# Linear attention and highway FFN: the last batch's queries turned by two DMA transposes, pair stores by every second partition, two thirds of the step list made anew

## The chip, the cores and the metric

The kernel runs on one core of one Trainium2 chip. The metric is device time in microseconds (us) of one execution. Engines are named as in the profile: PE is TensorE's matmul and PEld its weight load, DVE is VectorE, ACT is ScalarE, POOL is GpSimd, and SP is SyncE, which issues nearly all DMAs. L410 means line 410 of the kernel.

## The reference

```
# q, k, v: (8 batches, 8 heads, 576 positions, 64)
q_s = exp(q - max(q)) / sum over the last axis
k_s = exp(k - max(k)) / sum over the positions
kv  = einsum('bhsd,bhse->bhde', k_s, v)
x   = einsum('bhsd,bhde->bhse', q_s, kv), heads side by side: (4608, 512)
H   = max(x @ w_h, 0)
T   = 1 / (1 + exp(-(x @ w_t + b_t)))
out = T * H + (1 - T) * x          # (4608, 512), float32
```

The kernel leaves out the maxima (they cancel) and divides the query's exponentials only after the product with kv: a column of ones beside kv gives the sum.

## The kernel before

The 4608 rows of the output are 36 tiles of 128 rows. A batch has 576 positions, laid out as 64 partitions with 9 positions each, so two batches share nine tiles: four tiles of one batch, four of the other, and one mixed tile. Tiles 27 to 30 are batch 6, 31 to 34 batch 7, and tile 35, the last, has the ends of both; it is computed in two column halves.

Everything is cut into small steps. A step is one word of a list, ORDER, written out by a planner ahead of time: `xu_31_0` is step xu for tile 31, `:P`, `:A`, `:D` choose the engine, `:F` makes a step take a whole tensor in one instruction. The program issues the steps in that order, and every engine, SP's queue included, takes its own instructions strictly in that order. Waits come only from data and from buffers that are still in use (two PSUM banks each for tps and gps, one each for xu, qps and the turned x; three landing buffers each for q, k and v).

For a batch b:

- `q_b`, `k_b`, `v_b` (L183 to L205): loads in float32 on SP's queue. For batches 4 to 7 the queries come as a main part (`q_b_0`, two DMAs, L198) that fills 128 partitions with eight positions of every head, and the ninth positions (`q_b_9`, L202).
- `ek` (L252) and `vc` (L258): exponentials of k on ACT, the cast of v on any of three engines. `kv` (L268): 72 small matmuls; `kr`, `kn` (L280, L286): division on DVE into kvb.
- `eq` (L297 to L306): exponentials of q on ACT, into a tile qe of 16-bit values. `qt` (L318 or L323): TensorE transposes of qe into the PSUM bank qps, two groups of eight blocks of 128x128 and one small third group. `qc` (L332): a copy from PSUM to SBUF, on DVE or ACT, into eq. `turned_q` names the block of eq that a tile's step xu needs.

For a tile i:

- `xu` (L352): four or eight matmuls of eq's blocks with kvb. `rs`, `x` (L361, L367): division on DVE, giving x in 16 bits. `xt` (L375): four transposes on TensorE. `xe` (L382): their copy to SBUF, on DVE or ACT.
- `bw` puts the bias into a bank of tps, by a matmul (L392) or a copy on ACT (L390). `mt` (L402) adds x @ w_t, `mh` (L410) makes x @ (w_h - 1), four matmuls each.
- `th` (L424, L426): a tanh on ACT. `dd` (L430): a maximum on DVE. `uu`: (tanh + 1) times that, on DVE (L444) or, for `:P`, as two instructions on POOL (L441, L442). `oo` (L462): plus x, on POOL. `st` (L470 to L482): the store.

Tiles are stored in pairs where two neighbours have the same batch (4 KB in a row). For batches 0 to 3 a pair is stored by two DMAs of 256 KB, `st_i_0` from partitions 0 to 63 and `st_i_1` from 64 to 127 (L482). For batches 4 to 6 one DMA of 512 KB takes all 128 partitions (L478); the tiles of batch 7 and the mixed ones are stored alone.

`fill_n` (L167) issues n matmuls on zeros into an unused bank. They stand where TensorE would be idle.

Of the kernel before, what the change touches and what calls it, by code (L numbers as in the profile page):

```python
# [24 lines left out]
xu_4_1 kv_1_0 mt_2_0 kr_1_0 rs_4_1 eq_1_1 bw_5 th_2_0 kn_1_0 xu_5_0 eq_1_2 q_4_0 x_4_1 rs_5_0 x_5_0 mt_5_1 xu_4_0
qt_1_1 qc_1_1:A oo_0_0 v_4_0 xt_5_0 xe_5_0:D mh_5_1 uu_3_0:P bw_4 mh_5_0 rs_4_0 x_4_0 xt_4_1 xe_4_1:D mt_5_0 uu_2_0:P
oo_2_0 eq_2_0:F th_5_0 xu_6_0 dd_5 xt_4_0 xe_4_0:D qt_1_2 mh_4_1 mt_4_1 mt_4_0 th_4_0 oo_3_0 mh_4_0 bw_8:A rs_6_0
uu_5_0:P bw_6:A qc_1_2 ek_2_0:F x_6_0 xt_6_0 xe_6_0:D oo_5_0 xu_8_0 qt_2_0 rs_8_0 mh_6_0 q_4_9 x_8_0 dd_4 xt_8_0
xe_8_0:D xu_7_0 rs_7_0 qc_2_0 x_7_0 mt_6_0 dd_6 mt_8_0 vc_2_2:A qt_2_1 th_6_0 xt_7_0 qc_2_1:A th_8_0 vc_2_0 kv_2_0
mh_8_0 xe_7_0:D uu_6_0 kr_2_0 kn_2_0 mh_7_0 k_4_0 eq_3_0:F xu_9_0 dd_8 uu_4_0:P k_5_0 bw_7 qt_2_2 v_5_0 rs_9_0 oo_4_0  # L30
x_9_0 mt_7_0 xt_9_0 dd_7 qc_2_2:A q_5_0 xu_10_0 xe_9_0:D bw_10:A th_7_0 rs_10_0 x_10_0 oo_6_0 qt_3_0 qc_3_0 mh_9_0
bw_9:A ek_3_0:F uu_8_0:P uu_7_0:P vc_3_0 xu_12_0 st_1_1 xt_10_0 oo_8_0 rs_12_0 x_12_0 xe_10_0:D oo_7_0 mt_9_0 dd_9
qt_3_1 vc_3_2:A xu_11_0 xt_12_0 rs_11_0 x_11_0 xe_12_0:D mt_10_0 th_9_0 th_10_0 kv_3_0 uu_9_0 oo_9_0 xt_11_0 mh_10_0
xe_11_0 kr_3_0 kn_3_0 dd_10 mh_12_0 qc_3_1 xu_14_0 rs_14_0 x_14_0 bw_12:A bw_11:A mt_12_0 mh_11_0 uu_10_0:P oo_10_0
xu_13_0 eq_4_0 eq_4_1 qt_3_2 st_1_0 xt_14_0 vc_4_0 mt_11_0 dd_12 rs_13_0 th_12_0 x_13_0 qc_3_2 uu_12_0:P bw_14:A
oo_12_0 xu_15_0 rs_15_0 x_15_0 xe_14_0 th_11_0 qt_4_0 dd_11 mt_14_0 uu_11_0 xt_13_0 xu_16_0 rs_16_0 qc_4_0:A xe_13_0
x_16_0 mh_14_0 qt_4_1 xt_15_0 th_14_0 bw_13:A xu_17_0 xe_15_0:D mt_13_0 rs_17_0 x_17_0 ek_4_0:F mh_13_0 xt_16_0 eq_4_2
vc_4_2 th_13_0 k_6_0 kv_4_0 dd_14 dd_13 xe_16_0:D kr_4_0 kn_4_0 bw_15:A uu_13_0 mh_15_0 ek_5_0:F bw_16:A oo_11_0
vc_5_2:A mt_15_0 th_15_0 q_5_9 qc_4_1 xu_18_0 rs_18_0 x_18_0 v_6_0 dd_15 uu_14_0:P mh_16_0 xt_17_0 xe_17_0:D qt_4_2
mt_16_0 th_16_0 vc_5_0 dd_16 kv_5_0 oo_14_0 oo_13_0 kr_5_0 kn_5_0 qc_4_2:A mh_17_0 xt_18_0 xe_18_0:D bw_17:A uu_16_0  # L40
q_6_0 mt_17_0 eq_5_0:F xu_20_0 rs_20_0 mh_18_0 st_5_0 qt_5_1 x_20_0 dd_17 xt_20_0 bw_18:A st_3_1 th_17_0 xu_21_0
st_3_0 xe_20_0:D mt_18_0 qc_5_1:A uu_15_0:P bw_20:A rs_21_0 oo_15_0 st_5_1 x_21_0 qt_5_0 xt_21_0 dd_18 q_7_0 v_7_0
th_18_0 bw_21:A st_7_1 oo_16_0 xu_19_0 ek_6_0 uu_17_0:P oo_17_0 xe_21_0:D ek_6_2 rs_19_0 mh_20_0 mh_21_0 vc_6_0:A
x_19_0 xt_19_0 qc_5_0 xe_19_0:D xu_22_0 st_7_0 rs_22_0 x_22_0 dd_20 k_7_0 dd_21 mt_20_0 th_20_0 mt_21_0 vc_6_2
uu_18_0:P xt_22_0 kv_6_0 xe_22_0:D eq_5_2 mh_19_0 bw_19:A mt_19_0 qt_5_2 kr_6_0 kn_6_0 th_21_0 uu_21_0 xu_23_0 qc_5_2
eq_6_0:F mh_22_0 st_16_1 uu_20_0:P qt_6_0 bw_22:A st_10_1 rs_23_0 x_23_0 xt_23_0 xu_24_0 st_10_0 dd_19 mt_22_0
xe_23_0:D oo_18_0 oo_20_0 th_19_0 rs_24_0 oo_21_0 x_24_0 uu_19_0:P bw_23:A dd_22 mt_23_0 oo_19_0 qc_6_0 xt_24_0
xe_24_0:D st_21_0 xu_25_0 mh_23_0 q_6_9 rs_25_0 th_22_0 uu_22_0:P oo_22_0 mh_24_0 x_25_0 xt_25_0 dd_23 xu_26_0 dd_24
# [17 lines left out]
def kernel(  # L66
# [242 lines left out]
    def qt(e, b, g):  # L309
        j0, j1 = GROUPS[g]  # L310
        a, s = (2, 2) if g < 2 else (1, 1)
        t = T[f"qps{b}_{g}"] = ps_q.tile([P, a, 4, s, NP], FP16, tag="qps", name=f"qps_{b}_{g}")
        if b in WIDE and g < 2:
            main = T[f"qe{b}"].rearrange("p j c d -> p (j c d)")[:, 0:MAIN]
            main = main.rearrange("p (hh j kk f) -> p j hh kk f", j=4, hh=2, kk=2)
            for jp in (2 * g, 2 * g + 1):
                for n in range(4):
                    nc.tensor.matmul(t[:, jp % 2, n].rearrange("p s t -> p (s t)"), main[:, jp, n % 2, n // 2], idh,  # L318
                                     is_transpose=True, start=True, stop=True, skip_group_check=True)
# [8 lines left out]
    def qc(e, b, g):  # L328
# [3 lines left out]
        copy(t.rearrange("p a n t -> p (a n t)"), T[f"qps{b}_{g}"].rearrange("p a n s t -> p (a n s t)"))  # L332
# [192 lines left out]
```

## Time and profile before

| what | value |
|---|---|
| median of three runs | 119.64 us (119.22 to 120.39) |
| the profiled execution | 119.67 us |
| its span, first to last instruction | 117.6 us |
| moved by DMA | 40.06 MB, mean 341 GB/s |
| read from and written to HBM | 30.41 MB and 9.44 MB |
| TensorE's clock as granted | 1.000 |

The page has busy time by engine, DMA queues, and the chain of work that ended last, followed back from the last instruction. Other views are asked for with a window, a line or a tile: groups of instructions (busy time in all, mean ns of one, and behind the second bar the idle time of the engine just before them and what ended it), a timeline (start, duration, engine, line, operation), and busy time by windows (length, busy time and count for each engine, granted clock, DMA share, GB/s). Starts are counted from the first instruction of the span.

### The profile page before, as it was taken

The page shows a single profiled execution, that of the slowest core. Times are in us where ns is not written, and L with a number is a line of the kernel's source. Part 1 is how long each engine was busy: PE and PEld are TensorE (multiplying, and loading weights), DVE is VectorE, ACT ScalarE, POOL GpSimd, SP SyncE. Part 2 cuts the span into 40 slices and gives each one's busy share as a digit, 9 for nine tenths or more (in the row PEclk, how much of TensorE's full clock was granted, in tenths as well). Part 3 has the DMA queues.
Part 4 walks back from the last instruction along what each step waited for, and adds up shares of the span by engine and source line. Part 5 has one row for each costly group of instructions (what it writes and reads, how often), then busy time and mean ns, then how long its engine had stood idle before and what let it go on. Part 6 is the DMA issues. An engine that isn't in the chain of part 4 may idle for free.

```text
span 117.6 us, 3461 instructions
## 1 busy us (share of the span) xinstructions
PE 110.6 (94%) x1371; PEld 63.6 (54%) x1371; DVE 94.3 (80%) x223; ACT 92.3 (78%) x130; POOL 91.9 (78%) x103
## 2 busy tenths in 40 slices
...
GB/s 46 393 392 380 408 396 385 378 375 384 394 389 390 389 391 362 374 355 390 389 375 383 381 363 361 395 374 380 406 403 363 279 235 180 301 283 56 210 364 173
DMA packets 22083, 40.06 MB, mean 341 GB/s; under 512 B 3250, under 2 KB 9650, under 8 KB 22068
## 3 DMA queue, kind: packets, MB, share of 16 engines
q1 hardware_dynamic: 21920, 39.72, 94.8%
q8 instruction: 10, 0.16, 0.6%
...
HBM read 30.41 MB, written 9.44 MB: 339 GB/s over the span
## 4 chain that ended last, share of the span: by engine, by line
PE 69%; DMA 17%; DVE 8%; SPq 2%; ACT 1%; issue 1%; DVEq 0%
PE gps L410 23%; PE tps L402 22%; DMA q<-in_q_dram 11%; PE xu L352 6%; DMA v<-in_v_dram 6%; PE turned L375 5%; PE kv L268 4%; DVE x L367 4%; PE qps L323 2%; PE qps L318 2%; SPq L183 2%; PE turned L167 2%; DVE d L430 2%; ACT qe L306 1%; DVE rs L361 1%
## 5 line engine op out<-in xcount | busy, mean ns | idle before, releaser
L462 POOL TENSOR_TENSOR o<-u,x 128x512 f32<-128x512 f16 (+1 forms) x36 | 40.7, 1144 | 3.7 <-DVE u L444 2.8
L402 PE MATMUL tps<-w16t,xT 128*128 128x512 f16 (+1 forms) x148 | 36.3, 373 | 0.8 <-POOL w16t L221 0.8
L410 PE MATMUL gps<-w16h,xT 128*128 128x512 f16 x144 | 36.3, 379 | 0.0
L367 DVE TENSOR_TENSOR x<-xu,rs 128x512 f16<-128x512 f32 (+1 forms) x39 | 25.2, 649 | 2.8
L442 POOL TENSOR_TENSOR u<-g,d 128x512 f16<-128x512 f16 x21 | 24.3, 1157 | 2.5 <-DVE rs L361 0.9
L430 DVE SCALAR_TENSOR_TENSOR d<-x,gps 128x512 f16<-128x512 f16 x36 | 24.2, 678 | 1.7 <-PE gps L410 1.6
L252 ACT ACTIVATE ek<-k 128x576 f16<-128x576 f32 (+2 forms) x15 | 18.0, 1222 | 2.5 <-DMA k<-in_k_dram 2.5
L402 PEld LDWEIGHTS <-xT 128*128 128x128 f16 x148 | 13.4, 98 | 12.1 <-issue 1.1
L410 PEld LDWEIGHTS <-xT 128*128 128x128 f16 x144 | 12.8, 98 | 11.4 <-DVE xT L382 0.5
L390 ACT COPY tps<-ball 128x512 f32<-128x512 f32 x28 | 16.3, 592 | 2.4 <-DVE u L444 2.1
L258 POOL CAST v<-v 128x1152 f16<-128x1152 f32 (+1 forms) x10 | 9.5, 953 | 10.4 <-DMA v<-in_v_dram 9.9
L375 PE MATMUL turned<-idh,x 128*128 128x128 f16 x144 | 14.3, 220 | 1.0 <-DVE x L367 1.0
L352 PE MATMUL xu<-kvb,eq 128*128 128x130 f16 (+1 forms) x160 | 14.8, 224 | 0.5 <-DVE eq L332 0.2
L167 PE MATMUL turned<-blank 128*128 128x512 f16 x44 | 12.5, 431 | 1.3 <-POOL blank L149 1.3
L352 PEld LDWEIGHTS <-eq 128*128 128x128 f16 (+1 forms) x160 | 10.2, 100 | 6.5 <-DVE x L367 1.3
L424 ACT ACTIVATE th<-tps 128x512 f16<-128x512 f32 x21 | 12.3, 592 | 1.6 <-PE tps L402 1.6
L375 PEld LDWEIGHTS <-x 128*128 128x128 f16 x144 | 10.1, 98 | 6.5 <-DVE x L367 2.6
L441 POOL TENSOR_SCALAR g<-th 128x512 f16<-128x512 f16 x21 | 13.1, 622 | 0.2 <-ACT th L424 0.2
L382 DVE COPY xT<-turned 128x512 f16<-128x512 f16 (+1 forms) x27 | 10.8, 399 | 2.8 <-PE turned L375 2.5
L306 ACT ACTIVATE qe<-q 128x1024 f16<-128x1024 f32 (+2 forms) x8 | 9.2, 1160 | 4.3 <-DMA q<-in_q_dram 4.1
L426 ACT ACTIVATE tps<-tps 128x512 f32<-128x512 f32 (+1 forms) x16 | 8.9, 556 | 2.9 <-PE tps L402 2.7
L444 DVE SCALAR_TENSOR_TENSOR u<-tps,d 128x512 f16<-128x512 f32 (+1 forms) x15 | 10.0, 669 | 0.8 <-ACT tps L426 0.2
...
## 6 DMA issues: line engine op xcount, KB each, us to landing
k<-in_k_dram SPq DMA_DIRECT2D x6, 1152.0 KB, 11.6
...
out_dram<-o SPq DMA_DIRECT2D x23, 256.0 KB, 6.3
q<-in_q_dram SPq DMA_DIRECT2D x10, 512.0 KB, 9.5
out_dram<-o SPq DMA_DIRECT2D x6, 512.0 KB, 5.5
...
```

The source lines that it names most:

```text
L167: nc.tensor.matmul(spare, blank[:, 0:P], blank, start=True, stop=True, skip_group_check=True)
L252: nc.scalar.activation(t[:, :, c:c + n].rearrange("p j c d -> p c j d"), T[f"k32{b}"][:, c:c + n].rearrange("p c (j d) -> p c j d", j=NJ), ...
L352: nc.tensor.matmul(dst, turned_q(b, jp, n), kvb[b % NKV][:, hh, kk], start=True, stop=True, skip_group_check=True)
L367: nc.vector.tensor_mul(t[:, k0:k1], sums(i, k)[:, :, :, 0:64], T[f"rs{i}_{k}"][:, 0:k1 - k0].unsqueeze(3).to_broadcast([P, k1 - k0, 4, D]))
L375: nc.tensor.matmul(t[:, n], T[f"x{i}"][:, n0 + n % 2:n0 + 2 * P:2], idh, is_transpose=True, start=True, stop=True, skip_group_check=True)
L390: nc.scalar.copy(t[:, cs], ball[:, cs])
L402: nc.tensor.matmul(T[gate(i, k)][:, cs], T[f"xT{i}"][:, n], w16["t"][:, n, cs], start=False, stop=(n == parts[-1] and not first), skip_gro ...
L410: nc.tensor.matmul(t, T[f"xT{i}"][:, n], w16["h"][:, n], start=(first and n == parts[0]), stop=(n == parts[-1] and not (first and len(part ...
L430: nc.vector.scalar_tensor_tensor(t, T[f"x{i}"], -0.5, T[f"gps{i}"], op0=ALU.mult, op1=ALU.max)
L441: nc.gpsimd.tensor_scalar(g, T[f"th{i}"], 1.0, 1.0, op0=ALU.add, op1=ALU.mult)
L442: nc.gpsimd.tensor_mul(t, g, T[f"d{i}"])
L462: eng.tensor_add(t[:, cs], T[f"u{i}_{h}"][:, cs], T[f"x{i}"][:, cs])
```

## The change

Four things are edited.

1. `qt_7_0`, `qc_7_0`, `qt_7_1` and `qc_7_1` are gone: the eight main positions of batch 7's queries are no longer turned by TensorE and copied out of PSUM. Two new steps `qd_7_0` and `qd_7_1` are DMA transposes on SP's queue, each from half of qe (128x1024, 16 bits) straight to a tile of eq (eight blocks of 128x128). `turned_q` finds batch 7's blocks there: block n of a tile lies in half n % 2, so every tile of batch 7, from tile 31 on, reads both halves. The exponentials of batch 7 come in two halves, one for each transpose. The third group (`qt_7_2`, `qc_7_2`) stays.
2. For batches 0 to 3 the transposes by TensorE write their columns in another order in qps: a column stands for (position pair, which of two tile halves, which of the pair), where it was (half, position). The copy out is one plain row as before.
3. With that, the pair stores of batches 0 to 3 take every second partition (`o[h:P:2]`), 64 of them, again in rows of 4 KB.
4. The list has the same first 71 steps (up to `x_1_0`); the rest is another order. Steps move on every engine and on SP's queue. Engines change for some: nine `uu` go from POOL to DVE and five the other way; `vc_5_2`, `vc_6_0`, `vc_7_2` and `vc_7_0` go from ACT to POOL, `vc_1_2` from DVE to ACT; `qc_3_1`, `qc_4_1`, `qc_5_2` and `qc_6_1` go from DVE to ACT and `qc_4_0` the other way; four `xe` go to DVE and three to ACT; `bw_4` and `bw_7` go to ACT, `bw_8` and `bw_9` to TensorE. The exponentials of batches 2, 5, 6, 7 are issued in halves, those of batch 4 whole; of k, batch 3's are issued in halves and batch 6's whole. Six fills are added ahead of `xt_1_0`, and the ten behind the last matmul are gone.

```
-whd_3:P qc_0_1 xt_1_0 xu_3_0 qt_0_2 xe_1_0:D fill_1 rs_3_0 x_3_0 x_0_1 xt_3_0 xu_2_0 wtc_2:P whc_2:A mh_1_0 wtc_0:P
-vc_1_3 xe_3_0:D xt_0_0 xt_0_1 mh_3_0 qc_0_2:A xe_0_1 mt_1_0 mt_0_1 dd_1 ek_1_3 rs_2_0 xe_0_0:D mt_0_0 x_2_0 xt_2_0
-vc_1_2:D mh_0_0 th_1_0 mh_0_1 uu_1_0 dd_3 ek_1_2 kv_1_1 dd_0 th_0_0 oo_1_0 kr_1_1 kn_1_1 bw_3 eq_1_0 bw_2 qt_1_0
...
-rs_26_0 th_23_0 bw_24:A mt_24_0 x_26_0 eq_7_0:F uu_23_0:P qt_7_0 st_12_0 qc_7_0 xu_27_0 q_7_9 oo_23_0 rs_27_0 x_27_0
...
-mt_26_0 rs_28_0 ek_7_0:F dd_26 mt_27_0 oo_24_0 x_28_0 xt_29_0 kv_7_0 xe_29_0:D xt_28_0 th_26_0 uu_26_0 oo_26_0 th_27_0
-kr_7_0 kn_7_0 oo_25_0 bw_29:A mh_27_0 bw_28:A mh_29_0 dd_27 qc_7_1 xu_31_0 rs_31_0 xe_28_0 x_31_0 mt_29_0 eq_7_2
...
-rs_35_0 st_28_0 x_35_0 bw_34:A th_32_0 oo_30_0 st_30_0 dd_32 uu_32_0 oo_32_0 xt_35_0 xe_35_0 st_32_0 mt_34_0 bw_35_0
-mh_35_0 dd_34 bw_35_1 mt_35_0 th_34_0 uu_34_0 oo_34_0 th_35_0 st_34_0 mt_35_1 fill_6 dd_35 uu_35_0 th_35_1 uu_35_1
-oo_35_0 st_35_0 fill_4 oo_35_1:D st_35_1:A
+fill_6 whd_3:P qc_0_1 xt_1_0 xu_3_0 qt_0_2 qc_0_2:A xe_1_0:D fill_1 rs_3_0 x_3_0 x_0_1 xt_3_0 xu_2_0 rs_2_0 x_2_0
+wtc_2:P whc_2:A mh_1_0 wtc_0:P vc_1_3 ek_1_3 ek_1_2 vc_1_0 xe_3_0:D mh_3_0 dd_1 xt_0_1 xt_0_0 mt_1_0 xe_0_0:D mh_0_0
+xe_0_1 dd_3 xt_2_0 mh_0_1 mt_0_1 th_1_0 xe_2_0:D dd_0 vc_1_2:A kv_1_1 uu_1_0 oo_1_0 eq_1_0 mt_0_0 th_0_0 ek_1_0 ek_1_1
+kr_1_1 bw_3 qt_1_0 vc_1_1:A kn_1_1 qc_1_0 mt_3_0 xu_5_1 uu_0_0 mh_2_0 th_3_0 bw_2 rs_5_1 x_5_1 dd_2 xu_4_1 kv_1_0
...
+xt_23_0 xe_23_0:D k_7_0 mh_22_0 rs_24_0 bw_23:A x_24_0 mt_23_0 qc_6_0 xu_25_0 rs_25_0 x_25_0 st_10_0 uu_21_0:P oo_19_0
+xt_24_0 xe_24_0:D oo_21_0 mh_23_0 dd_22 uu_22_0:P xu_26_0 xt_25_0 oo_22_0 bw_24:A eq_7_0 mt_24_0 th_23_0 rs_26_0
+x_26_0 qt_6_1 xe_25_0 vc_7_2 qd_7_0 xt_26_0 xu_27_0 vc_7_0 mh_24_0 dd_23 uu_23_0 rs_27_0 eq_7_1 q_7_9 qd_7_1 st_17_0
+mh_25_0 x_27_0 qc_6_1:A bw_25:A xu_29_0 th_24_0 xe_26_0 dd_24 uu_24_0 mt_25_0 bw_26:A ek_7_0:F rs_29_0 x_29_0 th_25_0
+oo_23_0 mh_26_0 dd_25 xt_27_0 xu_28_0 rs_28_0 xe_27_0:D x_28_0 mt_26_0 bw_27:A st_8_0 xt_29_0 xe_29_0:D eq_7_2 q_6_9
+oo_24_0 mh_27_0 kv_7_0 dd_26 uu_25_0:P oo_25_0 th_26_0 xt_28_0 kr_7_0 mt_27_0 kn_7_0 mh_29_0 xe_28_0 dd_27 xu_31_0
+st_14_1 bw_28:A mt_28_0 th_27_0 st_12_0 bw_29:A mt_29_0 dd_29 th_28_0 eq_6_2 rs_31_0 x_31_0 st_25_0 xu_30_0 xt_31_0
...
+xt_35_0 mt_34_0 dd_32 th_32_0 bw_35_1 oo_30_0 st_16_0 st_30_0 uu_32_0 xe_35_0 oo_32_0 mh_35_0 th_34_0 bw_35_0 mt_35_0
+th_35_0 mt_35_1 dd_34 uu_34_0 oo_34_0 dd_35 uu_35_0 st_32_0 th_35_1 uu_35_1 st_34_0 oo_35_0 st_35_0 oo_35_1:D
+st_35_1:A
```

```diff
+    TURNED = (7,)
...
-        t = T[f"qps{b}_{g}"] = ps_q.tile([P, a, 4, s, NP], FP16, tag="qps", name=f"qps_{b}_{g}")
+        t = T[f"qps{b}_{g}"] = ps_q.tile([P, a, 4, s * NP], FP16, tag="qps", name=f"qps_{b}_{g}")
...
-                    t[:, (j - j0) % 2, 2 * kk:2 * kk + 2, (j - j0) // 2],
+                    t[:, (j - j0) % 2, 2 * kk:2 * kk + 2].rearrange("p n (t s u) -> p n t s u", s=s, u=2)[:, :, :, (j - j0) // 2],
...
+    def qd(e, b, g):
+        t = T[f"eq{b}_{g}"] = eqp.tile([P, 2, 4, P], FP16, tag="eq", name=f"eq_{b}_{g}")
+        half = MAIN // 2
+        nc.sync.dma_start_transpose(t.rearrange("p a n t -> p (a n) t"),
+                                    T[f"qe{b}"].rearrange("p j c d -> p (j c d)")[:, g * half:(g + 1) * half])
+
     def turned_q(b, jp, n):
+        if b in TURNED and jp < 4:
+            return T[f"eq{b}_{n % 2}"].rearrange("p a n t -> p (a n) t")[:, 2 * jp + n // 2]
         return T[f"eq{b}_{jp // 2}"][:, jp % 2, n]
...
-            j = 4 * (jp // 2) + 2 * h + (0 if both else jp % 2)
-            rows = out[b * S:(b + 1) * S].rearrange("(p j) n -> p (j n)", j=NJ)
-            eng.dma_start(rows[:, j * DM:j * DM + n], o[64 * h:64 * h + 64])
+            j = 4 * (jp // 2) + (0 if both else jp % 2)
+            dst = bass.AP(out.tensor, out.offset + (b * S + NJ * h + j) * DM, [[2 * NJ * DM, NP // 2], [2 * DM, 2], [1, n]])
+            eng.dma_start(dst, o[h:P:2])
```

More of the change, by code (lines that the diff above doesn't have):

```diff
@@ L25 @@
[L25 to L48, printed above, removed]
-rs_26_0 th_23_0 bw_24:A mt_24_0 x_26_0 eq_7_0:F uu_23_0:P qt_7_0 st_12_0 qc_7_0 xu_27_0 q_7_9 oo_23_0 rs_27_0 x_27_0
@@ new lines @@
+xe_12_0 bw_12:A mh_12_0 kr_3_0 qc_3_1:A kn_3_0 xu_14_0 rs_14_0 x_14_0 bw_11:A xt_11_0 xe_11_0 mt_12_0 th_12_0 qt_3_2
+v_6_0 xt_14_0 oo_9_0 k_6_0 xu_13_0 q_6_0 xe_14_0 mh_11_0 dd_12 qc_3_2 mt_11_0 rs_13_0 eq_4_0:F th_11_0 uu_12_0
+uu_10_0:P x_13_0 dd_11 xu_15_0 rs_15_0 vc_4_0 mh_14_0 x_15_0 st_5_1 dd_14 qt_4_0 oo_10_0 vc_4_2 xu_16_0 rs_16_0 x_16_0
+xt_13_0 xe_13_0:D oo_12_0 bw_14:A bw_13:A ek_4_0:F st_3_0 mt_14_0 th_14_0 xu_17_0 rs_17_0 bw_15:A x_17_0 qc_4_0
+xt_15_0 mt_13_0 kv_4_0 xe_15_0:D kr_4_0 uu_11_0:P oo_11_0 th_13_0 qt_4_1 uu_14_0:P st_3_1 mh_13_0 vc_5_2 xt_16_0
```

36 lines of the change are left out of this document (25 added, 11 removed).

## The prediction

> **What bounds the kernel now.** I read the page's first parts, then the chain of work that ended last, then busy time by windows cut at the chain's joints, then groups by shape, and last the timelines of ACT, SP and DVE near the changed steps.
>
> ```profile
> span 117.6 us, 3461 instructions
> PE 110.6 (94%) x1371; PEld 63.6 (54%) x1371; DVE 94.3 (80%) x223; ACT 92.3 (78%) x130; POOL 91.9 (78%) x103
> ...
> q1 hardware_dynamic: 21920, 39.72, 94.8%
> ```
>
> Two resources look full here, TensorE (94%) and the DMA engines (94.8% of their time on SP's queue). The chain says which one sets the end, and the windows say from when:
>
> ```profile
> 10.81 12.67 DMA q<-in_q_dram
> ...
> 23.50 1.06 ACT qe L306
> ...
> 24.61 0.62 PE qps L323 x8
> ...
> 86.44 0.45 PE qps L318 x8
> ...
> 90.84 0.45 PE qps L318 x8
> ...
> 111.99 0.87 PE tps L402 x8
> 112.86 2.16 PE turned L167 x10
> ```
>
> ```profile
> core 0: us, PE busy (x) PEld busy (x) DVE busy (x) ACT busy (x) POOL busy (x), PEclk, DMA share, GB/s
> 24.60:112.86 88.26, 87.99 (x1144) 52.91 (x1145) 78.23 (x175) 78.30 (x110) 82.09 (x84) 1.00 0.98 344
> ```
>
> The reader is to see three pieces. Up to 24.61 the kernel waits for batch 1's queries: the load issued at 10.81 lands at 23.47, ACT takes 1.06 for the exponentials, and only then qt_1_0 starts. From 24.61 to 112.86 TensorE shows 87.99 us busy of 88.26, so it sets the pace, at a granted clock of 1.00. From there to 117.6 there is a short tail. DMA is full too, but only as a supplier: it hurts when a load lands after its user wants it.
>
> Busy time hides small gaps, since a matmul's row includes its latency. The same stretch by groups:
>
> ```profile
> L402 PE MATMUL tps<-w16t,xT 128*128 128x512 f16 (+1 forms) x140 | 34.4, 373 | 0.0
> L410 PE MATMUL gps<-w16h,xT 128*128 128x512 f16 x132 | 33.3, 379 | 0.0
> L352 PE MATMUL xu<-kvb,eq 128*128 128x130 f16 (+1 forms) x144 | 13.2, 224 | 0.1
> L375 PE MATMUL turned<-idh,x 128*128 128x128 f16 x128 | 12.8, 220 | 0.0
> ```
>
> At the rate of the chain's back-to-back pieces (0.87 for eight half-width matmuls, so 0.215 for a full one; 0.45 for eight transposes, so 0.056 each) the 264 full matmuls make 56.8, the eight halves 0.9, the 128 transposes of x 7.2, the 144 of xu 8.1 (0.056 each as well), the 126 query transposes 7.1, and kv and the bias rows some 5: about 85.2 by the list. So about 3 us of the 88.25 are small gaps, not work. That is all that a better order could take out.
>
> **The change, part by part.** The sum is made against the profiled execution, 119.67 us (span 117.6, 2.07 around it); the median of the runs is 119.64, the same.
>
> Two query turns on TensorE go (qt_7_0, qt_7_1, sixteen transposes): the pieces at 86.44 and 90.84, 2 x 0.45 = 0.90, all inside the stretch where TensorE sets the pace. That is the gain. The bias matmul bw_2 now stands behind qt_1_0 instead of ahead of it: 0.22 more work in that stretch (two bias rows of the early list take 0.59 with one latency of some 0.16, so 0.22 each):
>
> ```profile
> 23.45 0.59 PE L392 MATMUL tps<-b,ones 128*128 128x512 f16 x2
> ```
>
> No other TensorE step crosses qt_1_0, and bw keeps its split between TensorE and ACT (two change each way). Sum on TensorE: -0.90 + 0.22 = -0.68.
>
> The other engines' moves are priced with these groups:
>
> ```profile
> L332 DVE COPY eq<-qps 128x1024 f16<-128x1024 f16 x12 | 8.2, 681 | 0.8 <-PE qps L323 0.4 <-PE qps L318 0.3
> L444 DVE SCALAR_TENSOR_TENSOR u<-tps,d 128x512 f16<-128x512 f32 x14 | 9.6, 686 | 0.7 <-ACT tps L426 0.2
> L332 ACT COPY eq<-qps 128x1024 f16<-128x1024 f16 x4 | 4.1, 1013 | 0.4 <-PE qps L318 0.2
> L258 ACT CAST v<-v 128x1152 f16<-128x1152 f32 x6 | 6.9, 1147 | 0.0
> L442 POOL TENSOR_TENSOR u<-g,d 128x512 f16<-128x512 f16 x21 | 24.3, 1157 | 2.5 <-DVE rs L361 0.9
> L441 POOL TENSOR_SCALAR g<-th 128x512 f16<-128x512 f16 x21 | 13.1, 622 | 0.2 <-ACT th L424 0.2
> L258 POOL CAST v<-v 128x1152 f16<-128x1152 f32 x6 | 6.9, 1144 | 0.3
> ```
>
> DVE gets four uu more (4 x 0.69) and loses qc_7_0 and qc_7_1, two qc on balance to ACT (4 x 0.68 in all), one small qc and one cast, with some 0.3 for copies of xT: about -0.7. ACT loses four casts of v to POOL (4 x 1.15), gains two large qc (2 x 1.01), vc_1_2, one small qc and some 0.5 for exponentials issued in halves, and gives 0.4 of copies of xT away: about -1.3. POOL loses four pairs of uu (4 x 1.78) and gains the four casts (4 x 1.14): about -2.5. None of the three becomes the bound; all get a little more air. This I put at nothing, because TensorE covers it. One wait is new on POOL: vc_1_0 now stands right behind vc_1_3 and ahead of oo_1_0, and its load is there only at about
>
> ```profile
> 26.60 0.66 POOL L258 CAST v<-v 128x576 f16<-128x576 f32 x1
> ```
>
> so POOL stands still from the end of vc_1_3 until 26.6. Behind it is oo_1_0, which only a store and a later tile of x wait for; uu_0, which the next TensorE steps are nearer to, has been moved to DVE. I take 0.
>
> Fills: six 512-wide fills are added ahead of xt_1_0, ten after mt_35_1 go. The ten stand behind the last matmul that anything waits for (chain: 112.86), so nothing is won. The six cost about 6 x 0.22 = 1.3 at some 14.3 us. Their cover is the wait for the cast of w_t:
>
> ```profile
> 19.00 1.04 POOL L221 CAST w16t<-w32t 128x1024 f16<-128x1024 f32 x1 [0.27 <-DMA w32t<-in_moe_w_t_dram]
> ...
> 20.09 1.89 PE L402 MATMUL tps<-w16t,xT 128*128 128x512 f16 x8 [0.83 <-POOL w16t L221]
> ```
>
> TensorE stands idle 0.83 there and again before 24.61. If that cover were gone it would be 1.3; I take 0.
>
> The layout in PSUM for batches 0 to 3 (pairs of columns four apart) costs nothing if a transpose into scattered columns takes as long as one into a plain row. Two layouts already stand side by side, with equal medians:
>
> ```profile
> L323 PE MATMUL qps<-idh,qe x80: 218/219/229, 6.4 to 98.7; 128*128 128x128 f16 x80
> L318 PE MATMUL qps<-idh,qe x64: 218/219/219, 54.4 to 91.1; 128*128 128x128 f16 x64
> ```
>
> So 0; the far end is twice the time for 62 of them, 62 x 0.056 = 3.5; no gain is possible, since nothing is faster than the plain row's 0.056.
>
> The pair stores of batches 0 to 3 stay sixteen DMAs of 256 KB in 4 KB rows, from every second partition in place of one half. The rows to read beside each other are those of stores that use half and all of the partitions:
>
> ```profile
> out_dram<-o SPq DMA_DIRECT2D x23, 256.0 KB, 6.3
> ...
> out_dram<-o SPq DMA_DIRECT2D x6, 512.0 KB, 5.5
> ```
>
> Twice the bytes land no later, so a half-partition store is not cheap now. If the new form helps, loads behind it land sooner; no step of TensorE waited visibly for a load after 24.61, so I take 0. The ends are nothing and, were each of the nine stores ahead of k_7_0 dearer by a whole one (0.67 at the rate below), 6 us on that load.
>
> Now the two DMA transposes, 256 KB each, an operation that no row shows. They stand on SP's queue behind k_7_0, st_10_0 and, for the second, q_7_9:
>
> ```profile
> L183 SPq DMA_DIRECT2D k<-in_k_dram x1: 586/586/586, 77.1 to 77.1; - x1
> ...
> DMA to landing us min/median/max: 11.6/11.6/11.6
> ```
>
> ```profile
> 80.00:90.00 10.00, 10.00 (x95) 6.27 (x94) 9.31 (x20) 8.33 (x12) 9.52 (x11) 1.00 1.05 393
> ```
>
> ```profile
> 96.13 0.40 PE L352 MATMUL xu<-kvb,eq 128*128 128x130 f16 x4
> ```
>
> k_7_0 landed at 77.1 + 11.6 = 88.7. By the list one more 256 KB store stands ahead of it now: 0.67 at 393 GB/s, so 89.4; st_10_0 brings the queue to 90.0. The lower end for a transpose is a plain 256 KB, 0.67. The upper end takes it as 1024 rows of 256 bytes at the mean time of a packet, 0.948 x 16 x 117.6 / 21920 = 0.081 us, over 16 engines: 5.2. The mean packet is seven times larger, so the lower end is nearer; I take twice it, 1.3, because data go in and out of SBUF. Then qd_7_0 lands at 91.3, q_7_9 (128 KB, 0.33) at 91.7, qd_7_1 at 93.0. Their first user is xu_31, which needs both: it started at 96.13, and 0.68 less work ahead makes 95.4. Cover 2.4; cost 0.
>
> The Trainium skill speaks against this in "VectorE: DVE Perf Modes", section "The three transpose paths": it gives 1309 ns for a 128x128 block by DMA and 390 ns on TensorE. Sixteen blocks one after another would be an estimate of 20.9 us from that page. Its page "DMA: Bandwidth & Descriptors", section "Latency and other measured facts", gives 261 GB/s for DMA transposes, an estimate of 1.0 us for each of ours, which would keep the sum as it is. No run here shows either yet.
>
> SP reaches qd_7_0 and waits there for eq_7_0; behind it wait q_7_9, stores, and q_6_9. Stores have slack, since what they free is used late. The other loads change places by one or two (v_4 ahead of q_4, v_6 ahead of k_6), their users by about as much; I price that in the third rival. q_7_9 does not: its user eq_7_2 moves 5.3 us of TensorE work forward in the list (from 94.7 to 89.4 counted from qt_1_0), so from 95.96 to about 90.7, against 91.7.
>
> ```profile
> 91.29 2.12 ACT L252 ACTIVATE ek<-k 128x2304 f16<-128x2304 f32 x1
> ...
> 95.96 0.72 ACT L297 ACTIVATE qe<-q 128x256 f16<-128x256 f32 x2
> ```
>
> ek_7_0 moves 2.85 forward too, to about 88.4, against k_7 at 89.4. So ACT waits about 1.0 twice. After ek_7_0's 2.12, kv_7 can start at 91.5, and its place is 93.51 - 0.68 = 92.8 (chain below): cover 1.3, where it was 2.7. I take 0.
>
> ```profile
> 93.51 0.72 PE kv L268 x69
> ```
>
> The tail keeps its order (mh_35, mt_35_0, mt_35_1; then th, uu, oo, store), so it keeps its 4.74. Sum: 119.67 - 0.68 = 118.99.
>
> **The rivals.** First, faster by order: three engines have 0.7 to 2.5 less to do, and half of the 3 us of gaps close: 119.0 - 1.5 = 117.5. For it, DVE, ACT and POOL all lose work; against it, the gaps that the profile shows as idle TensorE are only 0.27.
>
> Second, slower: the transposes come late for xu_31. This decides when both together take over 2.6 + 2.4 = 5.0, 2.5 each. At the upper end, 5.2 each, qd_7_1 lands at 90.0 + 10.4 + 0.33 = 100.7, TensorE, which takes its steps in order, stands for 5.3 from 95.4, and the kernel takes 124.3. For it: no row shows the operation, and small packets are dear. Against it: 2.4 of cover, and a queue that is past its loads.
>
> Third, slower by ACT: the two waits of 1.0 (k_7 and q_7_9 behind more traffic) pass on whole, because th_26, xe_28 and bw_28 stand behind them on ACT and mt_28 needs the last: 119.0 + 2.0 = 121.0. For it: both users move forward in the list while their loads do not. Against it: TensorE has kv_7, xt_28, mt_27, mh_29 and xu_31 to do meanwhile, some 2.9.
>
> Fourth, the transposes go block by block, sixteen after one another, each as long as two of the 0.67 moves: 21 us, landing at 90.0 + 21 + 0.33 = 111.3, 15.9 late, 134.9. The first page named above says about this. Nothing in the trace speaks for a transfer that does not spread over the 16 engines.
>
> That the change doesn't do what it says is no rival: the sixteen transposes are gone by the list.
>
> **How the numbers follow.** About 1% is what a measurement of this kernel can tell from no change (its three runs lie between 119.22 and 120.39). Forecast 119.0: 0.42, with a range of its own from 118.5 to 120.2. Faster by order (117.5): 0.25. ACT late (121.0): 0.20. Transposes late (124.3): 0.10. Block by block (134.9): 0.03. Faster by over 1% is the first rival, 0.25; within 1% the forecast, 0.42; slower the rest, 0.33. The range from 117.4 to 122.0 leaves out the last two cases, 0.13, and some edges.
>
> **What would show it.** Right: qps L318 with 48 in place of 64; a first qps of batch 1 again near 24.6; TensorE without a gap before xu_31 (about 95.4); the last matmul near 112.2; each transpose landing within some 4 us of its issue with the queue then empty of loads. Wrong: TensorE's weight load idle at L352 on a DMA into eq (second rival); ACT idle at L252 or L297 on DMA with TensorE idle behind (third); or qt_1_0 later than 24.6, which would mean that the fills or the early order cost after all.

## The result, and the profile after

| | median (all runs) | ratio to before |
|---|---|---|
| before, beside it | 119.64 us (15 runs) | |
| the changed kernel | 118.80 us (15 runs) | 0.9925 [0.9906, 0.9945] |

The changed kernel is 0.75% faster, inside the "within 1%" case and 0.2 us from the forecast of 119.0. Ratios, here and below, compare undisturbed runs alone; a median beside one is over all runs of that kernel.

The page's first parts, after:

```profile
span 116.9 us, 3424 instructions
...
PE 109.5 (94%) x1351; PEld 61.6 (53%) x1351; DVE 93.3 (80%) x222; ACT 90.0 (77%) x132; POOL 89.1 (76%) x99
```

TensorE is busy for the same share of a shorter span, and DMA is fuller (96.9% of the engines' time on SP's queue, was 94.8%). The other three engines lost work as predicted: DVE 1.0 (predicted 0.7), POOL 2.8 (2.5), and ACT 2.3, which is 1.0 more than the 1.3 predicted; that difference was not traced.

Busy time of the stretch in which TensorE sets the pace, and in it the group of batch 4 to 7's query transposes:

```profile
24.60:112.20 87.60, 87.47 (x1129) 51.05 (x1128) 77.19 (x172) 76.23 (x113) 80.41 (x80) 1.00 1.01 355
```

```profile
L319 PE MATMUL qps<-idh,qe 128*128 128x128 f16 x48 | 3.7, 219 | 0.0
```

Matmuls still fill the stretch (87.47 of 87.60), and 48 transposes stand where 64 stood. The timeline's rows for the first piece of the stretch (qt_1_0), its last (mt_35, both halves), and the last oo:

```profile
24.57 0.62 PE L324 MATMUL qps<-idh,qe 128*128 128x128 f16 x8
...
111.05 1.04 PE L411 MATMUL tps<-w16t,xT 128*128 128x256 f16 x8
...
113.06 0.42 DVE L471 TENSOR_TENSOR o<-tps,x 128x256 f32<-128x256 f32 x1
```

From qt_1_0 to mt_35 the trace of before has 24.61 to 111.83, 87.22; after has 86.48. So the span's change of 0.7 is this stretch: -0.74. The start moved by -0.04, the way from mt_35 to the last oo by 0.01 (2.01 after 2.00), and from there to the end by +0.07 (3.84 after 3.77). The profiled execution took 118.69, so another 0.28 of its difference to 119.67 lies outside the span.

### The profile page after: what moved, and what is told of

The parts are those of the page before. It is cut to its first block, busy times and chain, and to the rows that moved or that the text cites. A ratio compares the mean times of both kernels' runs of the same rounds, so it can differ in the third digit from the quotient of the medians.

```text
span 116.9 us, 3424 instructions
## 1 busy us (share of the span) xinstructions
PE 109.5 (94%) x1351; PEld 61.6 (53%) x1351; DVE 93.3 (80%) x222; ACT 90.0 (77%) x132; POOL 89.1 (76%) x99
## 2 busy tenths in 40 slices
DMA packets 24195, 40.58 MB, mean 347 GB/s; under 512 B 5362, under 2 KB 11762, under 8 KB 24180
## 3 DMA queue, kind: packets, MB, share of 16 engines
q1 hardware_dynamic: 24032, 40.24, 96.9%
## 4 chain that ended last, share of the span: by engine, by line
PE 67%; POOL 15%; issue 6%; DVE 5%; DMA 3%; SPq 1%; POOLq 0%; DVEq 0%
PE tps L411 18%; PE gps L419 16%; PE turned L167 9%; POOL o L471 7%; PE xu L361 6%; PE turned L384 5%; PE kv L269 5%; PE qps L324 4%; POOL u L451 4%; DMA out_dram<-o 3%; POOL g L450 2%; PE qps L319 2%; POOL v L259 2%; DVE x L376 2%; PE tps L401 1%
## 5 line engine op out<-in xcount | busy, mean ns | idle before, releaser
L411 PE MATMUL tps<-w16t,xT 128*128 128x512 f16 (+1 forms) x148 | 37.3, 373 | 0.0
L419 PE MATMUL gps<-w16h,xT 128*128 128x512 f16 x144 | 36.8, 379 | 0.5 <-DVE xT L391 0.5
L259 POOL CAST v<-v 128x1152 f16<-128x1152 f32 (+1 forms) x14 | 14.0, 1010 | 14.7 <-DMA v<-in_v_dram 13.7
L451 POOL TENSOR_TENSOR u<-g,d 128x512 f16<-128x512 f16 x17 | 19.7, 1158 | 1.7 <-DVE rs L370 0.4
L435 ACT ACTIVATE tps<-tps 128x512 f32<-128x512 f32 (+1 forms) x20 | 11.2, 559 | 3.6 <-PE tps L411 3.3
L453 DVE SCALAR_TENSOR_TENSOR u<-tps,d 128x512 f16<-128x512 f32 (+1 forms) x19 | 12.7, 671 | 1.4 <-ACT tps L435 0.6
L307 ACT ACTIVATE qe<-q 128x1024 f16<-128x1024 f32 (+3 forms) x9 | 9.4, 1052 | 4.1 <-DMA q<-in_q_dram 4.1
L450 POOL TENSOR_SCALAR g<-th 128x512 f16<-128x512 f16 x17 | 10.6, 621 | 0.9 <-ACT th L433 0.9
L433 ACT ACTIVATE th<-tps 128x512 f16<-128x512 f32 x17 | 10.0, 594 | 0.9 <-PE tps L411 0.9
## 6 DMA issues: line engine op xcount, KB each, us to landing
q<-in_q_dram SPq DMA_DIRECT2D x2, 640.0 KB, 10.5
```

Source lines behind the costliest of these rows:

```text
L259: copy(v16[b % NV][:, c:c + n, :, 0:D], T[f"v32{b}"][:, c:c + n].rearrange("p c (j d) -> p c j d", j=NJ))
L411: nc.tensor.matmul(T[gate(i, k)][:, cs], T[f"xT{i}"][:, n], w16["t"][:, n, cs], start=False, stop=(n == parts[-1] and not first), skip_gro ...
L419: nc.tensor.matmul(t, T[f"xT{i}"][:, n], w16["h"][:, n], start=(first and n == parts[0]), stop=(n == parts[-1] and not (first and len(part ...
L451: nc.gpsimd.tensor_mul(t, g, T[f"d{i}"])
```

## The experiments

All twelve kernels ran in five rounds beside the kernel before (medians of 119.61 to 119.75 in these calls). The theory: sixteen transposes leave a stretch that TensorE paces (-0.9), and the rest of the change is about neutral. Rivals: the new order brings the gain; the new stores do; the transposes by DMA cost something that the order hides.

**One profile's error.** The order-only kernel below and the changed kernel differ by 0.92 in that stretch; how far may two profiles differ by chance? e6 and e9, below, have the same list up to xu_26, yet reach it 60.38 and 60.84 after qt_1_0. That is the old list. The new one repeats better: the changed kernel, e3, e5, e7, e10 and e12 have it unaltered up to xu_26 and reach it after 59.49 to 59.57. So a stretch of the old list is good to about 0.4, one of the new list to about 0.1, and smaller differences are read only where a wait or the spacing of two steps shows them.

### e1 and e5: the new list and stores, but batch 7 still turned by TensorE

```diff
-    TURNED = (7,)
+    TURNED = ()
```

In e1 the four steps of batch 7 come back into the new list where there seemed to be room: qt_7_0 behind xu_29, qc_7_0 behind xe_26, qt_7_1 behind mh_29, qc_7_1 behind dd_27.

> The changed kernel with its new list and new pair stores, but batch 7's queries turned by TensorE and copied by DVE again: both DMA transposes out, the two groups of eight TensorE transposes and two copies (0.68 us each on DVE) back in. Theory of the work (the gain is the 0.90 us of TensorE work taken away, less 0.22 for a bias row, and the order itself gives nothing): 0.90 us over the changed kernel's 118.8, so 119.7, ratio to before about 1.00. Rival of the order (the new list closes gaps, the transposes hardly matter): 118.8 to 119.0, ratio 0.993 to 0.995.

Measured: 121.76 us, ratio 1.0175 [1.0142, 1.0207]. This is more than sixteen transposes can cost, and the timelines of DVE and PE show the greater part of why:

```profile
89.46 0.69 DVE L333 COPY eq<-qps 128x1024 f16<-128x1024 f16 x1 [1.02 <-PE qps L319]
```

```profile
90.80 1.02 PE L419 MATMUL gps<-w16h,xT 128*128 128x512 f16 x4 [0.51 <-DVE d L439]
...
92.50 0.41 PE L361 MATMUL xu<-kvb,eq 128*128 128x130 f16 x4 [0.46 <-DVE x L376]
```

DVE takes its list in order and came to the copy before TensorE had made the transposes; it stood 1.02, and TensorE then stood 0.97 for DVE (0.51 + 0.46), of the 1.66 by which its stretch is longer than that of e5. The run tells of the place that I chose, not of the order. e5 places the steps anew: qt_7_0 behind mt_25, qc_7_0 behind x_29, qt_7_1 behind mt_27, qc_7_1 behind dd_27.

> Again the changed kernel with batch 7 turned by TensorE, with the four steps at other places: qt_7_0 behind mt_25, qc_7_0 behind x_29, qt_7_1 behind mt_27, qc_7_1 behind dd_27, so that DVE need not wait for TensorE in front of dd_24. Theory of the work: 118.8 + 0.90 = 119.7, ratio 1.000, with no idle of DVE in front of the copies. Rival (the new list is good only where those steps are out, DVE has no room for 2 x 0.68 there): again over 121.

Measured: 119.86 us, ratio 1.0022 [1.0000, 1.0044]; from qt_1_0 to mt_35 87.40. New order and new stores without the DMA transposes gain nothing. Against it the changed kernel has 0.92 less in the stretch, and by the ends of the two intervals 0.7 to 1.7 us less time. PE's timeline of e5 has xu_26 and xu_31, the steps around the places of the four TensorE steps, at

```profile
84.18 0.42 PE L361 MATMUL xu<-kvb,eq 128*64 128x130 f16 x8
...
96.51 0.40 PE L361 MATMUL xu<-kvb,eq 128*128 128x130 f16 x4
```

which is 12.33 apart; in the changed kernel they are 11.40 apart (84.07 and 95.47, below). So the 0.93 lies just where the TensorE transposes stand in e5, and up to xu_26 the two kernels take 59.49 and 59.50. The rival of order falls.

### e2, e6 and e9: the transposes alone, in the old list

e2 is the kernel before with qd added; qt_7_0, qc_7_0, qt_7_1 and qc_7_1 go.

```
-... eq_7_0:F uu_23_0:P qt_7_0 st_12_0 qc_7_0 xu_27_0 q_7_9 ...
+... eq_7_0:F uu_23_0:P qd_7_0 qd_7_1 st_12_0 xu_27_0 q_7_9 ...
```

> The kernel before, list, layout and stores as they were, with one edit: batch 7's two groups of TensorE transposes and their copies go, and two DMA transposes are issued behind the exponentials. Theory of the work: 119.64 - 0.90 = 118.7, ratio 0.9925, last matmul some 0.9 earlier. Rival of the order: 119.6, ratio 1.00. Rival of the late transposes (they need a list made for them): over 120, with the weight load of xu_31 idle on a DMA into eq.

Measured: 121.68 us, ratio 1.010 [1.0057, 1.0143]. Slower: the same two operations that win about 1% in the new list (from e5 to the changed kernel) lose 1.0% in the old one. The twelve times scatter from 119.93 to 123.82, and the profiled execution, 119.99, is one of the fastest, so what follows is read from a mild case; what the slowest ones wait for is not in a trace. SP's timeline and ACT's:

```profile
86.00 7.19 SPq L340 DMA_TRANSPOSE eq<-qe  x2
...
93.87 0.59 SPq L203 DMA_DIRECT2D q<-in_q_dram  x1
```

```profile
97.11 0.72 ACT L298 ACTIVATE qe<-q 128x256 f16<-128x256 f32 x2 [0.87 <-DMA q<-in_q_dram]
```

Two transposes hold SP's queue for 7.19 us (4.40 for the first, 2.68 for the second). q_7_9, behind them, is issued at 93.87, and ACT stands 0.87 for it. That is the mechanism of the third rival, brought about by SP's issuing and not by landing. e6 only moves q_7_9 ahead:

```
-... uu_23_0:P qd_7_0 qd_7_1 st_12_0 xu_27_0 q_7_9 oo_23_0 ...
+... uu_23_0:P q_7_9 qd_7_0 qd_7_1 st_12_0 xu_27_0 oo_23_0 ...
```

> The kernel before with the two DMA transposes, as in the run of the transposes alone, but q_7_9 issued ahead of them. The wait of ACT for q_7_9 (0.87 us in that run) should go. If that wait was what ate the gain: 118.8, ratio 0.993. If TensorE, with sixteen transposes less, instead waits for DVE where those transposes used to stand (xu_27 waits for x_26 through the one bank of xu; two such waits of 0.2 us in that run, more in its weight loads): 119.3 to 119.8, ratio 0.997 to 1.001.

Measured: 119.64 us, ratio 0.9987 [0.9954, 1.0019]. ACT's wait is gone, and with it e2's loss, but 0.9 is not gained. Look at the xu steps around the two places where the transposes stood. PE's timeline of before (xu_26, transposes, xu_27; then xu_29, transposes, xu_28, in the list's order):

```profile
85.04 0.43 PE L352 MATMUL xu<-kvb,eq 128*64 128x130 f16 x8
...
86.28 0.61 PE L318 MATMUL qps<-idh,qe 128*128 128x128 f16 x8
86.72 0.40 PE L352 MATMUL xu<-kvb,eq 128*128 128x130 f16 x4
...
89.35 0.40 PE L352 MATMUL xu<-kvb,eq 128*128 128x130 f16 x4
...
90.68 0.61 PE L318 MATMUL qps<-idh,qe 128*128 128x128 f16 x8
91.12 0.40 PE L352 MATMUL xu<-kvb,eq 128*128 128x130 f16 x4
```

The same four xu steps in e6:

```profile
84.76 0.43 PE L361 MATMUL xu<-kvb,eq 128*64 128x130 f16 x8
...
86.36 0.41 PE L361 MATMUL xu<-kvb,eq 128*128 128x130 f16 x4 [0.20 <-DVE x L376]
...
89.00 0.40 PE L361 MATMUL xu<-kvb,eq 128*128 128x130 f16 x4
...
90.70 0.41 PE L361 MATMUL xu<-kvb,eq 128*128 128x130 f16 x4 [0.21 <-DVE x L376]
```

With eight transposes in between, the distances were 1.68 and 1.77; without them they are 1.60 and 1.70. Each group of 0.45 gave 0.08 or 0.07, and over the whole way from xu_26 to xu_31 the two of them gave 0.07 (11.09 before, 11.02 in e6): xu has one PSUM bank, the next xu may start only when DVE has made x from the last, and the transposes had filled that round trip. (In before no wait is shown there: TensorE arrived just in time, with work that is now gone.) e9 puts other work in the first of the two places, the transposes of batch 6's second group:

```
-... st_12_0 xu_27_0 oo_23_0 ... st_17_0 qt_6_1 qc_6_1 ...
+... st_12_0 qt_6_1 xu_27_0 oo_23_0 ... st_17_0 qc_6_1 ...
```

> The kernel before with the transposes behind q_7_9, as e6, and in the list one more edit: the TensorE transposes of batch 6's second group (qt_6_1) stand ahead of xu_27 instead of later, so that TensorE has work in one of the two places that the removed transposes left empty. Theory of the empty places: the wait of TensorE for DVE's x ahead of xu_27 (0.20 us shown, with the DVE lateness behind it) goes, the one ahead of xu_28 stays, and about 0.4 us is gained on e6: 119.2 us, ratio 0.995 to 0.997. Rival, that the order of the list in those places doesn't matter: 119.6 us again, ratio 0.999, and the wait ahead of xu_27 either stays or moves to the next place.

Measured: 119.33 us, ratio 0.9975 [0.9937, 1.0013]. PE's timeline, from xu_26 to xu_28:

```profile
85.25 0.42 PE L361 MATMUL xu<-kvb,eq 128*64 128x130 f16 x8
...
86.48 0.61 PE L319 MATMUL qps<-idh,qe 128*128 128x128 f16 x8
86.92 0.40 PE L361 MATMUL xu<-kvb,eq 128*128 128x130 f16 x4
...
90.86 0.41 PE L361 MATMUL xu<-kvb,eq 128*128 128x130 f16 x4 [0.25 <-DVE x L376]
```

The first wait is gone, the second stays, and the way from xu_26 to xu_28 takes 5.61 where e6 took 5.94: 0.33 won, near the 0.4 expected. Up to xu_31 0.24 of that is left (10.78 where e6 took 11.02), and there the weight load waits 0.25 for a DMA into eq, a first small sign of the second rival. The timed runs lean the same way (0.3 in the medians), but their intervals overlap and don't prove it.

### e7: each transpose issued twice

The changed kernel, with each qd first issued into a tile that nothing reads.

```diff
+        junk = once("junk", lambda: consts.tile([P, 2, 4, P], FP16, name="junk"))
+        nc.sync.dma_start_transpose(junk.rearrange("p a n t -> p (a n) t"),
+                                    T[f"qe{b}"].rearrange("p j c d -> p (j c d)")[:, g * half:(g + 1) * half])
```

> The changed kernel with each DMA transpose issued twice, first into a tile that nothing reads, then as before; the output is unchanged. It doubles the disputed cost. By the prediction's prices (1.3 us each, cover 2.4) both real ones would land 2.6 later and the end moves by 0.2: 119.0. By what the changed kernel's trace shows (each held SP's queue for 3.0 to 3.3 us) they land about 6 later, q_7_9 3 later, and TensorE waits in front of xu_31: 121 to 123, with ACT idle on q or the weight load of xu idle.

Measured: 119.72 us, ratio 0.9990 [0.9966, 1.0013], 0.9 over the changed kernel and under what I expected. SP's timeline, and PE's at xu_31:

```profile
83.00 3.06 SPq L341 DMA_TRANSPOSE junk<-qe  x1
86.18 3.59 SPq L343 DMA_TRANSPOSE eq<-qe  x1
...
90.91 1.81 SPq L341 DMA_TRANSPOSE junk<-qe  x1
92.82 1.25 SPq L343 DMA_TRANSPOSE eq<-qe  x1
```

```profile
95.51 0.22 PE L364 MATMUL xu<-kvb,eq 128*128 128x130 f16 x1
96.04 0.35 PE L364 MATMUL xu<-kvb,eq 128*128 128x130 f16 x3 [0.31 <-DMA eq<-qe]
```

The second rival's sign holds TensorE up here: xu_31 waits for a DMA into eq, up to 96.04. The useful second transpose, issued at 92.82, landed by then, about 3.2 us after its issue. It is issued 6.06 later than in the changed kernel (86.76, below), and yet it holds TensorE up by only about half a microsecond. More comes from what stands behind the transposes on SP's queue. POOL's timeline and DVE's:

```profile
102.43 2.26 POOL L474 TENSOR_TENSOR o<-u,x 128x512 f32<-128x512 f16 x2 [1.63 <-DMA out_dram<-o]
```

```profile
103.61 0.69 DVE L379 TENSOR_TENSOR x<-xu,rs 128x512 f16<-128x512 f32 x1 [0.66 <-POOL o L474]
```

A late store keeps its buffer from POOL for 1.63, POOL keeps x's buffer from DVE for 0.66, and xu_34 waits for DVE: xu_32 starts 0.67 later than in the changed kernel, xu_34 0.94, xu_35 and mt_35 1.21. The first two issues, ahead of 87 us, take 3.06 and 3.59, the last two, behind 90 us, 1.81 and 1.25.

### e3, e8, e10, e12: the pair stores

e3 is the changed kernel with the old stores and the old column order in qps; e8 is the kernel before with the new ones.

```diff
-            dst = bass.AP(out.tensor, out.offset + (b * S + NJ * h + j) * DM, [[2 * NJ * DM, NP // 2], [2 * DM, 2], [1, n]])
-            eng.dma_start(dst, o[h:P:2])
+            eng.dma_start(rows[:, j * DM:j * DM + n], o[64 * h:64 * h + 64])
```

> The changed kernel with the pair stores of batches 0 to 3 from half of the partitions again, and the columns in PSUM in the old order. Theory of the work: no difference, 118.8, ratio 0.993, since TensorE and not DMA sets the pace after 24.6 us; the 256 KB stores land later again (median 6 us in place of 4.0) and k_7 lands up to 1 us later. Rival of the stores (their relief of the DMA queue is what pays): 119.3 or more, with ACT idle on the exponentials of k or q.

> The kernel before with the new pair stores and the new order of columns in PSUM alone. Its last pair store goes out at 97.6, long before the end, so the cheaper stores have nothing to shorten in the drain: 119.6 to 119.7, ratio 1.000. Rival of the stores (their relief of the DMA queue during the loads is worth time by itself): 119.2 or less, ratio 0.996.

Measured: e3 119.31 us, 0.9966 [0.9945, 0.9988]; e8 119.52 us, 0.9995 [0.9968, 1.0021]. In the old list the form of the stores makes no measurable difference; in the new one the old form costs 0.4 to 0.5. The rival's number came, but not its way: ACT waits 1.1 for loads of q in e3 and 0.6 in the changed kernel (1.0 in e5, with new stores), and TensorE doesn't feel it: from qt_1_0 to mt_35 e3 takes 86.46, as the changed kernel (86.48). So the loss lies behind TensorE: from the last oo to the end e3 takes 4.2, the changed kernel 3.84. The new list holds one such store, st_16_0, back to the end; SP issues it at 109.44 in e3 and at 109.32 after. The stretch from 108 to 118 us in 40 slices of 0.25, first e3:

```profile
DMA  9999991089999999259999999999996200000000
GB/s 426 377 426 352 369 369 58 0 303 393 369 295 229 229 131 180 82 229 442 377 426 377 385 418 377 344 401 361 332 348 238 74 0 0 0 0 0 0 0 0
```

and the changed kernel:

```profile
DMA  9989950299998999999990019999990000000000
GB/s 410 393 344 385 385 213 0 82 393 393 426 442 344 443 410 426 393 393 344 385 344 25 0 49 328 360 377 324 336 312 12 0 0 0 0 0 0 0 0 0
```

In e3 the engines are full in the slices from 110.75 to 112.0 but move 131 to 295 GB/s; after, the same slices move 344 to 443. From issue to landing the store takes 3.5 us in e3 and 2.5 after:

```profile
DMA to landing us min/median/max: 3.5/7.8/11.7
```

```profile
DMA to landing us min/median/max: 2.5/7.8/11.6
```

(stores of L491; the minimum is st_16_0's.) The stores issued behind it, at 111 to 113 us, take 2.8 to 3.6 us to land in e3 and 2.4 to 2.6 after. The Trainium skill says in "SBUF — State Buffer", section "Door 1: The DMA port swizzle", that partitions 0 to 63 reach only 8 of 16 ports. The trace agrees: about half of the rate with busy engines, while that store is on its way. e10 tests the place: e3 with st_16_0 right behind st_16_1, some nine microseconds earlier; e12 does that to the changed kernel.

```
-xt_30_0 xe_30_0 xu_33_0 st_16_1 oo_27_0 ...  oo_30_0 st_16_0 st_30_0 ...
+xt_30_0 xe_30_0 xu_33_0 st_16_1 st_16_0 oo_27_0 ...  oo_30_0 st_30_0 ...
```

> The changed kernel with the old pair stores (64 neighbouring partitions for each tile) as in e3, but with st_16_0 issued right behind st_16_1 rather than at the end of the list. Theory of the last drain: the 0.5 us that e3 lost against the changed kernel lies in a 256 KB store that is issued at 109.4 us and takes 3.5 us to land rather than 2.5; issued earlier it is out of the way, and the time is that of the changed kernel, 118.8 to 119.0 us, ratio 0.993 to 0.995. Rival, that the old stores cost through the whole span: 119.3 us again, ratio 0.997.

> The changed kernel, its new stores kept, with st_16_0 issued right behind st_16_1, as in e10. It completes the table of two store forms by two places of st_16_0. Theory of the last drain: with the new form the late store already lands in 2.5 us and there is next to nothing left to gain, 118.7 to 118.9 us, ratio 0.992 to 0.993, the same as the changed kernel. Rival, that the place of this store matters for itself by the same 0.4 us as with the old form: 118.4 us, ratio 0.989.

| | st_16_0 late | st_16_0 early |
|---|---|---|
| new stores | 118.80, 0.9925 [0.9906, 0.9945] | 118.93, 0.9938 [0.9915, 0.9960] |
| old stores | 119.31, 0.9966 [0.9945, 0.9988] | 118.80, 0.9931 [0.9907, 0.9956] |

Three of four are alike; only the old form at the end of the drain is slower. Its interval touches that of the changed kernel and overlaps those of the early stores by 0.0011 and 0.0015, so it is the trace above that makes this the cause and not the times alone. The new stores are not needed for the gain: they repair what the new list's late st_16_0 would cost.

### e4 and e11: early fills and the bias matmul

e4 is the changed kernel without `fill_6` ahead of xt_1_0. e11 is e4 with `bw_2:A`, so the bias is put in by ACT.

> The changed kernel without the six fills ahead of xt_1_0. If the wait for batch 1's queries covers them, as predicted: no difference, 118.8, ratio 0.993, qt_1_0 again at 24.6. Rival (the early TensorE work had no cover left: in the changed kernel's chain TensorE runs without a gap from 22.9 into qt_1_0 at 24.6): some 0.3 to 0.9 faster, 117.9 to 118.5.

> The changed kernel without its early sixth fill (e4 showed that to cost nothing) and with the work of bw_2 on ACT as a copy instead of on TensorE. Theory of the sum of work: TensorE's 0.22 us for bw_2 leave its bound stretch, and the time is 118.6 us, ratio 0.991. Rival: ACT is busy between 25 and 31 us, the copy there makes the queries' or the keys' activations late, TensorE waits for them, and the time is 118.8 to 119.2 us, ratio 0.993 to 0.996.

Measured: e4 118.90 us, 0.9930 [0.9903, 0.9956]: the fills cost nothing, as predicted. e11 119.04 us, 0.9953 [0.9927, 0.9979]: no gain, so no version found here beats the changed kernel. The timelines of PE and PEld from qt_1_0 to the second xu, in e4 and then e11:

```profile
24.89 0.62 PE L324 MATMUL qps<-idh,qe 128*128 128x128 f16 x8
...
27.29 0.38 PE L401 MATMUL tps<-b,ones 128*128 128x512 f16 x1
27.57 0.11 PEld L361 LDWEIGHTS <-eq 128*128 128x128 f16 x2 [0.39 <-DVE x L376]
```

```profile
24.76 0.62 PE L324 MATMUL qps<-idh,qe 128*128 128x128 f16 x8
...
27.44 0.11 PEld L361 LDWEIGHTS <-eq 128*128 128x128 f16 x2 [0.61 <-DVE x L376]
```

With the bias matmul or without it, that xu starts with its weights 2.68 behind qt_1_0. It waits for DVE's x, and without bw_2 the wait is 0.22 longer: bw_2 lay in a gap, and without it the gap stays. What e11's rival foresaw shows too: ACT's copy of the bias runs from 27.73 to 28.32, and the next matmul with w_t starts at 28.37, 0.29 behind the transposes ahead of it where e4 has 0.12.

## Why the prediction was right, and where it was not

**Sum.** -0.68 predicted for the stretch, -0.74 measured. The first term, -0.90 for sixteen transposes, is borne out by e5 against the changed kernel: 0.92 in the stretch, and in time 0.7 to 1.7. That the whole sum came so near is in part luck: its second term and its zero for the stores were not what the runs show (below), and the old list, which it starts from, takes 87.22 in one profile and 87.52 in another (e8).

**The step under that term was incomplete.** I wrote that the transposes were "all inside the stretch where TensorE sets the pace" and took their full length for a gain. e2 and e6 show that this does not follow: in the old list both groups stood where TensorE would have waited for DVE's x, and only 0.07 of the 0.90 came out. I had even worked out 3 us of small gaps, but not asked whether the removed work was filling one. It pays in the new list because there other work stands between the xu steps (PE's timeline after, xu_26, xu_27, xu_29, xu_28):

```profile
84.07 0.43 PE L361 MATMUL xu<-kvb,eq 128*64 128x130 f16 x8
...
86.20 0.40 PE L361 MATMUL xu<-kvb,eq 128*128 128x130 f16 x4
86.44 1.89 PE L419 MATMUL gps<-w16h,xT 128*128 128x512 f16 x8
88.30 0.39 PE L361 MATMUL xu<-kvb,eq 128*128 128x130 f16 x4
...
90.51 0.41 PE L361 MATMUL xu<-kvb,eq 128*128 128x130 f16 x4
```

The distances are 2.13, 2.10 and 2.21, all over the 1.60 to 1.70 that DVE's round trip takes, and none of the last three waits for DVE's x, on its matmuls or on its weight loads (that of xu_29 waits 0.44 for ACT). So order and transposes gain together what neither does alone (e5 1.0022, e6 0.9987).

**The second term, +0.22 for bw_2, is not borne out.** e11 finds that matmul in a gap. e5's stretch is 0.18 longer than before's, but that is within what the old list differs by itself, so whether the other -0.74 + 0.92 = 0.18 is anything stays open.

**The transposes.** I put each at 1.3 us on a queue that is through with its loads at 90.0. SP's timeline after, and the landing of L340:

```profile
82.96 3.00 SPq L340 DMA_TRANSPOSE eq<-qe  x1
...
86.76 3.32 SPq L340 DMA_TRANSPOSE eq<-qe  x1
```

```profile
DMA to landing us min/median/max: 7.9/7.9/7.9
```

SP issues them from 82.96 and is held for 3.00 and 3.32; the first lands at 82.96 + 7.9 = 90.9 (predicted 91.3; the second's landing is not in the trace). The landing was right, the price was not: I had priced what the queue moves and not what SP needs to issue it. Held for 6.3 in all, over the 5.0 that I gave as the second rival's condition, SP was still through in time, because it issued ahead of 90.0, while k_7 was on its way (landed at 89.2, predicted 89.4). That 6.3 did no harm is luck in that I had not reckoned with it. The cover at xu_31, 2.4 by my landing of 93.0, stays open, since that landing is missing; e7 shows that an issue 6.06 later is only about 0.5 too late. Of the stores behind I wrote that they have slack; e7 shows that the slack ends. The fourth rival is out: eight blocks landed 7.9 us after their issue with k_7 ahead of them, and 3.2 us after it in e6, where the rule in the Trainium skill ("VectorE: DVE Perf Modes", "The three transpose paths") of 1309 ns for a block would give an estimate of 10.5.

**ACT's waits.** Predicted were two of 1.0, for k_7 and q_7_9. ACT's timeline has none:

```profile
90.11 2.12 ACT L253 ACTIVATE ek<-k 128x2304 f16<-128x2304 f32 x1
...
93.27 0.41 ACT L298 ACTIVATE qe<-q 128x256 f16<-128x256 f32 x1
```

I moved each step by the TensorE work that it passed in the list (to 88.4 and 90.7). ACT has its own list, and its own work brought it there at 90.11 and 93.27, behind the landings of k_7 at 89.2 and of q_7_9 at 91.4 (predicted 91.7). That is why the third rival did not come; e2 shows that it was real, with q_7_9 behind both transposes.

**Steps right as told.** kv_7 and xu_31 on PE's timeline:

```profile
92.80 0.78 PE L269 MATMUL kv<-v,ek 64*64 64x65 f16 x72
...
95.47 0.40 PE L361 MATMUL xu<-kvb,eq 128*128 128x130 f16 x4
```

Predicted were 92.8 and 95.4. POOL's new wait ended at 26.56 (predicted 26.6); it stood 3.86 there, and nothing on TensorE followed from it. The fills cost nothing (e4), and qt_1_0 kept its 24.6. The first rival, half of the gaps closed by order, did not come: e5.

**Stores at 0.** Right in the old list as far as can be measured (e8), and wrong by 0.4 to 0.5 in the new one (e3), where the row that I compared, the median landing of all 256 KB stores, hides the one store at the end for which nothing else keeps the engines' rate up. For the sum it cancelled: I had neither the late st_16_0's price nor the new form's gain in it.
